# One stationary operand for the high and low parts of 64 tokens, a slot for each gated tile, and a new order of steps in a fused attention kernel

## The chip, the cores and the metric

The kernel runs on 1 core of one Trainium2 chip. The metric is the device time of one execution in microseconds, as the median of three runs. Work is spread over TensorE (PE in the profile, with its weight loads as PEld), VectorE (DVE), ScalarE (ACT), GpSimd (POOL) and the DMA engines, whose transfers are issued by SyncE (SP) and, for a few, by ACT.

## The reference, cut to what matters

Eight batches go through three blocks, each in float32:

- attention of 8 heads through 32 packed queries: `pp = softmax(p k^T) v`, then `softmax(q pp^T) pp`, for 576 tokens of 512 numbers (`x`);
- a gated MLP: `h = gelu(x w_in)`, halves `u` and `v`, `vn` = `v` normalised, `vs = w_sg vn + b_sg`, `x2 = x + (u * vs) w_out`;
- a mixture of 4 experts over causal attention: `logits = x2 w_gate`, the best two experts per token, `q, k, v = x2 wq, x2 wk, x2 wv` for each expert, and `out = sum of weight * softmax(q k^T) v wo`.

## The kernel before

**Tiles.** The 576 tokens are four tiles of 128 and one of 64. Factors are split into a rounded high part (float32r) and the low part that is left; a product takes three passes, high by high, high by low and low by high (`PASSES`). The weights of the third block are folded with `w_out`, so that `qk` and `vlog` come from the gated tiles `g` (four of 128 features, `m` = 0 to 3, with 576 tokens in each, times `w_qk` or `w_vg`) and from the packed attention `a2` (two halves `Q`, times `bd` or `bdv`, which `bdw` makes anew for each batch).

**Loops.** One batch after the other: `front(b)` makes `v` and its normalisation and `u`; `back(b)` makes `vs`, the gated tiles, `qk`, `vlog` and the gates, beside the attention steps of the batch before (S scores and softmax with E and N as its halves, T transposes, y and o the products) and the packed attention of the next one (K, s, n, a, p, P, Q, r). Batch 0 has a startup of its own (`ORDER`) and `first_back`, the others `later_back`; the last batch's attention is the tail of the program, in `back` at `b + 1 == B`.

**Order.** PE and SP run in the order of the program text (`tc.manual_schedule`). The startup's text orders all engines. Elsewhere DVE, ACT and POOL are ordered by a planner that simulates the program, except in blocks that name an engine. `prep_w_o` (loads, casts and splits the output weights) stands at the end of batch 0's back; its `lo_part` runs on POOL.

**Names that the change touches.** `gate_high` (L797) gives the gated tiles two by two a high and a low slot of tag `A`, and casts on ACT; `gate_low` (L805) subtracts on DVE. `vlog` (L861) makes, for a group of token tiles, 256 columns of values and 4 of logits: 12 matmuls from `g` (L871) and 6 from `a2` (L875) for each tile, a copy on ACT (L877) and one on DVE (L880), the latter twice for the tile of 64, to fill both halves of the partitions. `gates` (L882) follows the last `vlog`. `keep_last_q` (L855) copies on POOL what the last 64 queries need. `scores` of s is L392, its maximum L479 and exponential L481; `a1T` turns them (L501, copied at L503); `bdw` is L636. `v_pow` (L679) on POOL, `v_scale` (L683) and `v_low` (L698, L700) on DVE belong to the normalisation. The line of `lo_part` is L85, that of `act_copy` L82, both helpers. PSUM tiles are all of one tag, `pd`, with four slots.

Of the kernel before, what the change touches and what calls it, by code (L numbers as in the profile page):

```python
# [17 lines left out]
P = 128  # L18
# [8 lines left out]
def packed_attention_mlp_moe_kernel(  # L27
# [34 lines left out]

    NB = {"A": 4, "B": 10, "C": 4, "D": 12, "a": 3, "p": 2, "T": 4, "nat": 2, "t": 4, "v2": 1, "y": 1, "W": 2}
    NPS = 4
    BY = {"A": 1152, "B": 576, "C": 640, "D": 576, "a": 1152, "p": 576, "T": 512, "t": 576, "W": 2048}

    def slot(tag, dt=F32, w=None, name=None):
        t = sb.tile([P, BY[tag]], dt, tag=tag, name=name or ("s" + tag), bufs=NB[tag])
# [5 lines left out]
    def pd(name):  # L74

        return psum.tile([P, 2, 512], F32, tag="pd", name=name, bufs=NPS)
# [7 lines left out]
    def lo_part(eng, o, x, hi):  # L84
        eng.tensor_tensor(o, x, hi.bitcast(F32), op=OP.subtract)  # L85
# [548 lines left out]
        wp_out(b, f)  # L634

    def bdw(b):  # L636

        s = ST[b]
        pt = pd("bdq")
        per_head(b, pt, 512, w_of(b, "qk"))  # L640
        for Q in range(2):
            hi, lo = s["bd", Q] = [slot("B", F32R, 512, name="bdq") for _ in range(2)]
            nc.scalar.activation(hi, pt[:, Q, :], AF.Copy)
            lo_part(nc.vector, lo, pt[:, Q, :], hi)
        pt = pd("bdv")
        per_head(b, pt, 260, w_of(b, "vg"))
        t = [slot("B", F32R, 520, name="bdv").rearrange("p (q n) -> p q n", q=2) for _ in range(2)]
        nc.scalar.activation(t[0], pt[:, :, :260], AF.Copy)
        lo_part(nc.vector, t[1], pt[:, :, :260], t[0])
        for Q in range(2):  # L650
            s["bdv", Q] = [x[:, Q, :] for x in t]
# [144 lines left out]

    def gate_high(b, m):  # L797
        s = ST[b]
        if ("gt2", m // 2) not in s:
            s["gt2", m // 2] = (slot("A", F32R, name="gh"), slot("A", F32R, name="gl"))  # L800
        a = (m % 2) * S
        s["g", m] = [t[:, a:a + S] for t in s["gt2", m // 2]]
        nc.scalar.activation(two(s["g", m][0]), s["gt", m], AF.Copy)

    def gate_low(b, m):  # L805
        s = ST[b]
        hi, lo = s["g", m]
        lo_part(nc.vector, two(lo), s.pop(("gt", m)), two(hi))

    def qk(b, i):  # L810
        qk_mm(b, i)
# [48 lines left out]
    def vlog(b, cs):  # L860
        s = ST[b]  # L861
        if "v2" not in s:
            s["v2"] = sb.tile([P, NT, 256], F32, tag="v2", name="v2", bufs=NB["v2"])
            s["lg"] = small.tile([P, NT, E], F32, name="lg", bufs=2)
        n = TOK[cs[0]]
        k = len(cs)
        pt = pd("vlog")
        for ci, c in enumerate(cs):
            for m in range(4):
                for x, y in PASSES:  # L870
                    nc.tensor.matmul(pt[:n, ci, :260], s["g", m][x][:, c * P:c * P + n], W["w_vg"][y][:, m, :],  # L871
                                     start=(m, x, y) == (0, 0, 0), stop=False)
            for Q in range(2):
                for x, y in PASSES:
                    nc.tensor.matmul(pt[:n, ci, :260], s["a2", Q][x][:, c * P:c * P + n], s["bdv", Q][y],  # L875
                                     start=False, stop=(Q, x, y) == (1, 1, 0))
        nc.scalar.activation(s["v2"][:n, cs[0]:cs[0] + k, :], pt[:n, :k, :256], AF.Copy)  # L877

        for o in range(0, P, n):
            nc.vector.tensor_copy(s["lg"][o:o + n, cs[0]:cs[0] + k, :], pt[:n, :k, 256:260])  # L880

    def gates(b):  # L882
        s = ST[b]
# [1 line left out]
        T4 = [P, NT, E, E]  # L885
        other = lg[:, :, None, :].to_broadcast(T4)
        mine = lg[:, :, :, None].to_broadcast(T4)
        cmp = small.tile(T4, F32, name="cmp", bufs=1)
        eq = small.tile(T4, F32, name="eq", bufs=1)
        nc.vector.tensor_tensor(cmp, other, mine, op=OP.is_gt)  # L890
        nc.vector.tensor_tensor(eq, other, mine, op=OP.is_equal)
        nc.vector.tensor_tensor(eq, eq, tri[:, None, :, :].to_broadcast(T4), op=OP.mult)
# [224 lines left out]

    def first_back(b, do_all):
        tick(len(TURN))
        do_all("K0")  # L1120
        qk_gated(b, 0, True)
        do_all("s0 n0 K1 V")
        qk_gated(b, 2, True)
        do_all("s1 n1")
        bdw(b)
        weights(b + 1, ("in1", "in0"))
        do_all("a0")
        qk_packed(b, 0, False)
        qk_out(b, 0)
        do_all("a1 p0 Q0")  # L1130
        qk_packed(b, 2, False)
        qk_out(b, 2)
        keep_last_q(b, 0)
        do_all("P0")
        vlog(b, VT[2])
        do_all("p1 Q1 P1")
        vlog(b, VT[1])
        do_all("r")
        ahead(b + 2)

    def later_back(b, go, do_all, nxt):
        go("S1 S3")
        vs_tile(b, 0)
        vs_tile(b, 1)
        go("T1 T2 y0 S5 S4")
        vs_tile(b, 2)
        go("T3 o0 y1 T5 T4 S6 S7")
        vs_tile(b, 3)
# [30 lines left out]
    def back(b, go):  # L1179
# [16 lines left out]
        if b + 1 == B:  # L1196
            with tc.manual_schedule(engines={ET.DVE}):
                nxt("N8 N6")
                qk(b, 1)
                keep_last_q(b, 1)  # L1200
                nxt("E2 N4")
                qk_packed(b, 3, True)
                nxt("E0 N2")
                qk_gated(b, 3, False)
                qk_out(b, 3)
                nxt("N0 T8 T0 T2 E9 E1 T4 N9 E3 T6 N1 T9 y4 N3 T1 E5 y0 o4 T3 y1 N5 E7 o0 T5 y2 N7 o1 T7 y3 o2 o3")
            return
        qk(b, 1)
        keep_last_q(b, 1)
# [12 lines left out]
            qk_out(b, 3)  # L1222
            nxt("N0 N2")
        weights(b + 1, ("qk", "vg"))
        if b == 0:
            for j in range(2):
                prep_w_o(j)
        return nxt

    def ahead(b):  # L1230
# [294 lines left out]
```

## Time and profile before

| what | value |
|---|---|
| median of 3 runs | 844.61 us (844.15 to 848.43) |
| the profiled execution's own time | 844.43 us |
| its span, first to last instruction | 842.7 us |
| PE busy / PEld busy | 804.4 us (95%) / 695.5 us (83%) |
| DVE / ACT / POOL busy | 572.3 us (68%) / 431.1 us (51%) / 226.1 us (27%) |
| mean granted clock of TensorE | 0.992 |

A batch takes 94.5 us in its steady state. The busy time of PE counts matmuls whose durations overlap; where it is near the whole of a stretch, look in the timeline for the gaps that are left, which stand in brackets with what ended them. Times in the rows are microseconds from the span's start.

### The profile page before, as it was taken

The numbers are of one execution on the slowest core, as the hardware profiler recorded it, in microseconds if no ns is written. First come the engines' busy times: TensorE is split into PE (matmuls) and PEld (weight loads), VectorE is DVE, ScalarE is ACT, GpSimd is POOL, SyncE is SP. The second block draws the span as 40 slices with busy tenths as digits, with TensorE's granted clock in tenths as the row PEclk, the third lists the DMA queues.
The fourth block names the chain that finished last, engine by engine and source line by source line (L and its number), as shares of the span: only waits on it lengthen the run. The fifth ranks groups of instructions, "written<-read, shape, count | busy, mean of one in ns | idle before, by whom it ended". The sixth has DMA issues, their size and how long they took to land.

```text
span 842.7 us, 19253 instructions
## 1 busy us (share of the span) xinstructions
PE 804.4 (95%) x7523; PEld 695.5 (83%) x7523; DVE 572.3 (68%) x1359; ACT 431.1 (51%) x983; POOL 226.1 (27%) x301
## 2 busy tenths in 40 slices
PE   4689989999999999999999999999999999999988
PEld 2467778788889889888889889888889889888876
DVE  5999546776468846776468856776468856775374
ACT  3655432765347542665346542665346543665344
POOL 2457412403322322303322331303322322300000
PEclk9989999999999999999999999999999999999999
DMA  9977793617555374517565475617654470200001
GB/s 249 284 202 170 221 272 92 190 50 214 141 153 121 95 231 113 165 51 217 136 163 113 101 226 112 160 56 214 147 161 108 99 228 8 76 14 27 19 1 58
DMA packets 172710, 115.00 MB, mean 136 GB/s; under 512 B 119306, under 2 KB 153610, under 8 KB 169804
## 3 DMA queue, kind: packets, MB, share of 16 engines
q1 hardware_dynamic: 165644, 112.19, 49.7%
q10 hardware_dynamic: 6976, 1.58, 0.9%
q8 instruction: 60, 0.98, 0.5%
q14 instruction: 30, 0.25, 0.1%
HBM read 69.18 MB, written 29.63 MB: 117 GB/s over the span
## 4 chain that ended last, share of the span: by engine, by line
PE 59%; DVE 14%; ACT 4%; issue 3%; ACTq 0%
PE qk L828 10%; PE vlog L871 6%; PE vs L772 6%; PE y L1011 6%; PE qk L840 6%; PE o L1060 5%; PE aTp L982 4%; PE vlog L875 3%; PE sc L924 3%; DVE vg L683 2%; DVE bnst L671 2%; DVE vnl L698 2%; PE s L392 2%; PE sc L955 2%; DVE at L943 1%
## 5 line engine op out<-in xcount | busy, mean ns | idle before, releaser
L772 PE MATMUL vs<-w_sg,vnh 128*128 128x288 f32 x512 | 91.7, 301 | 3.4 <-ACT aT L82 1.9
L473 POOL COPY kT<-kp 128x576 uint16<-128x576 uint16 x56 | 50.2, 973 | 157.6 <-DMA kp<-turned_k 132.3
L828 PE MATMUL qk<-gh,w_qk 128*128 128x288 f32 x512 | 90.6, 299 | 0.0
L772 PEld LDWEIGHTS vs<-w_sg,vnh 128*128 128x128 f32 x512 | 74.5, 188 | 10.7 <-issue 3.9
L934 ACT ACTIVATE at<-sc,nm 128x256 f32<-128x256 f32 (+3 forms) x128 | 66.1, 524 | 32.4 <-DVE nm L928 28.6
L828 PEld LDWEIGHTS qk<-gh,w_qk 128*128 128x128 f32 x512 | 74.7, 188 | 9.3 <-issue 9.3
L82 ACT ACTIVATE aT<-aTp 128x512 f32<-128x512 f32 (+4 forms) x160 | 59.3, 434 | 21.1 <-PE aTp L982 17.7
L858 POOL CAST last_q<-qk 64x64 fp32r<-64x64 f32 x64 | 14.9, 232 | 178.4 <-ACT qk L848 101.6
L871 PE MATMUL vlog<-w_vg,gh 128*128 128x260 f32 (+1 forms) x320 | 60.5, 287 | 0.0
L473 POOL COPY qT<-qp 128x576 uint16<-128x576 uint16 x56 | 42.8, 833 | 62.0 <-DMA qp<-turned_q 61.9
L1011 PE MATMUL y<-aT,v 128*64 128x128 f32 (+2 forms) x960 | 57.7, 262 | 0.2 <-DVE y L85 0.2
L679 POOL TENSOR_TENSOR rstd<-rstd,mhalf 128x1 f32<-128x1 f32 x40 | 35.5, 894 | 83.2 <-DVE rstd L675 83.2
L1011 PEld LDWEIGHTS y<-aT,v 128*64 128x64 f32 (+1 forms) x960 | 46.7, 136 | 12.2 <-issue 7.3
L943 DVE TENSOR_SCALAR at<-at,sm,gw 128x256 f32<-128x256 f32 (+3 forms) x128 | 54.8, 470 | 1.6
L828 PE MATMUL qk<-gl,w_qk 128*128 128x288 f32 x256 | 54.8, 296 | 0.0
L772 PE MATMUL vs<-w_sg,vnl 128*128 128x288 f32 x256 | 54.7, 295 | 0.0
L928 DVE TENSOR_REDUCE nm<-sc 128x2 f32<-128x256 f32 (+3 forms) x64 | 52.0, 821 | 1.5
L871 PEld LDWEIGHTS vlog<-w_vg,gh 128*128 128x128 f32 (+1 forms) x320 | 47.2, 178 | 3.9 <-DVE lg L880 2.8
L1060 PE MATMUL o<-w_o,y 128*128 128x512 f32 x186 | 50.0, 404 | 0.0
L840 PE MATMUL qk<-a2h,bdq 128*128 128x288 f32 x256 | 46.8, 305 | 0.0
L982 PE MATMUL aTp<-ident,at 128*128 128x128 f32 x320 | 43.6, 274 | 2.7 <-DVE at L943 2.3
L871 PE MATMUL vlog<-w_vg,gl 128*128 128x260 f32 (+1 forms) x160 | 45.1, 282 | 0.0
(237 smaller groups left out, 1922.9 us busy)
## 6 DMA issues: line engine op xcount, KB each, us to landing
w_in<-kept_in SPq DMA_DIRECT2D x14, 1024.0 KB
w_qk<-kept_qk SPq DMA_DIRECT2D x8, 1024.0 KB
turned_k<-kx SPq DMA_DIRECT2D x28, 288.0 KB
turned_q<-qx SPq DMA_DIRECT2D x28, 288.0 KB
kp<-turned_k SPq DMA_DIRECT2D x56, 144.0 KB
qp<-turned_q SPq DMA_DIRECT2D x56, 144.0 KB
out_dram<-ot SPq DMA_DIRECT2D x31, 256.0 KB
v<-in_v_dram SPq DMA_DIRECT2D x56, 128.0 KB
```

Source lines behind the costliest of these rows:

```text
L82: nc.scalar.activation(o, i, AF.Copy, scale=scale)
L473: nc.gpsimd.tensor_copy(w[:, i], t[:, i].rearrange("p h n -> p (h n)"))
L772: nc.tensor.matmul(pt[:, h, :], s["vn", c][x][:, cols], w_sg[y][:, c, hs(h)], start=(c, x, y) == (0, 0, 0), stop=False)
L828: nc.tensor.matmul(o[:, h, :], W["w_qk"][y][:, m, cols], s["g", m][x][:, hs(h)], start=first and (m, x, y) == (0, 0, 0), stop=not first an ...
L840: nc.tensor.matmul(o[:, h, :], s["bd", Q][y][:, cols], s["a2", Q][x][:, hs(h)], start=first and (Q, x, y) == (0, 0, 0), stop=not first and ...
L871: nc.tensor.matmul(pt[:n, ci, :260], s["g", m][x][:, c * P:c * P + n], W["w_vg"][y][:, m, :], start=(m, x, y) == (0, 0, 0), stop=False)
L928: nc.vector.tensor_reduce(nm, pt[:, :, :L], axis=AX.X, op=OP.max, negate=True)
L934: nc.scalar.activation(ats[e][:, :L], pt[:, e, :L], AF.Exp, bias=nm[:, e:e + 1], accum_out=sm[:, e:e + 1])
L943: nc.vector.tensor_scalar(ats[e][:, :L], ats[e][:, :L], sm[:, e:e + 1], s["w"][:, j, 2 * pr + e:2 * pr + e + 1], op0=OP.mult, op1=OP.mult)
L982: nc.tensor.transpose(pt[:, e, c * P:c * P + P], ats[e][:, c * P:c * P + P], ident)
L1011: nc.tensor.matmul(pt[64 * e:64 * e + 64, pr * w:pr * w + w], s["v2"][:m, c, col:col + D], s["aT", pr, e, j][c][:m, :], start=c == 0, stop ...
L1060: nc.tensor.matmul(pt, ys[:, pr, x, :], W["w_o"][y][:, pr, :], start=i == 0, stop=i == 5)
```

## The change

It has six parts.

1. **One slot per gated tile.** Each `m` gets one `A` slot of 1216 numbers: the high part (576), room for 64, the low part (576). `gate_low` copies the low part's last 64 columns into that room, on ACT, so that the last 64 tokens' high and low parts lie side by side.
2. **The 64-token tile of `vlog`.** One matmul with those 128 columns as stationary operand gives high by high and low by high at once, in the two halves of the partitions; a second one, with the 64 high columns, gives high by low. From `g` it is 8 matmuls in place of 12. The halves are then added: a copy on ACT and an addition on DVE for the values, a copy and an addition on DVE for the logits, and a copy on POOL fills the other half.
3. **`first_back`** has a new order: `V` ahead of `K0`, both score steps together, `bdw` in two parts, with DVE in the text's order for the middle of it.
4. **`prep_w_o`** moves from the end of batch 0's back to ahead of the steps that fetch batch 2.
5. **`later_back`** orders ACT as T1, T2, then the gating of the second `vs` tile.
6. **The tail** has N0 ahead of `qk_out(b, 3)`, and T2, T4 and the E steps earlier.

Beside these, `gates` takes its two scratch tiles from the tag `rem`.

```diff
@@ -62,7 +62,7 @@
 
     NB = {"A": 4, "B": 10, "C": 4, "D": 12, "a": 3, "p": 2, "T": 4, "nat": 2, "t": 4, "v2": 1, "y": 1, "W": 2}
     NPS = 4
-    BY = {"A": 1152, "B": 576, "C": 640, "D": 576, "a": 1152, "p": 576, "T": 512, "t": 576, "W": 2048}
+    BY = {"A": 1216, "B": 576, "C": 640, "D": 576, "a": 1152, "p": 576, "T": 512, "t": 576, "W": 2048}
 
     def slot(tag, dt=F32, w=None, name=None):
         t = sb.tile([P, BY[tag]], dt, tag=tag, name=name or ("s" + tag), bufs=NB[tag])
@@ -634,7 +634,10 @@
         wp_out(b, f)
 
     def bdw(b):
-
+        bdw_qk(b)
+        bdw_vg(b)
+
+    def bdw_qk(b):
         s = ST[b]
         pt = pd("bdq")
         per_head(b, pt, 512, w_of(b, "qk"))
@@ -642,6 +645,9 @@
             hi, lo = s["bd", Q] = [slot("B", F32R, 512, name="bdq") for _ in range(2)]
             nc.scalar.activation(hi, pt[:, Q, :], AF.Copy)
             lo_part(nc.vector, lo, pt[:, Q, :], hi)
+
+    def bdw_vg(b):
+        s = ST[b]
         pt = pd("bdv")
         per_head(b, pt, 260, w_of(b, "vg"))
         t = [slot("B", F32R, 520, name="bdv").rearrange("p (q n) -> p q n", q=2) for _ in range(2)]
@@ -796,16 +802,15 @@
 
     def gate_high(b, m):
         s = ST[b]
-        if ("gt2", m // 2) not in s:
-            s["gt2", m // 2] = (slot("A", F32R, name="gh"), slot("A", F32R, name="gl"))
-        a = (m % 2) * S
-        s["g", m] = [t[:, a:a + S] for t in s["gt2", m // 2]]
+        t = s["gx", m] = slot("A", F32R, name="g")
+        s["g", m] = [t[:, :S], t[:, S + 64:]]
         nc.scalar.activation(two(s["g", m][0]), s["gt", m], AF.Copy)
 
     def gate_low(b, m):
         s = ST[b]
         hi, lo = s["g", m]
         lo_part(nc.vector, two(lo), s.pop(("gt", m)), two(hi))
+        act_copy(s["gx", m][:, S:S + 64], lo[:, 512:].bitcast(F32))
 
     def qk(b, i):
         qk_mm(b, i)
@@ -867,17 +872,28 @@
         pt = pd("vlog")
         for ci, c in enumerate(cs):
             for m in range(4):
+                if n < P:
+                    for y, k in ((0, P), (1, n)):
+                        nc.tensor.matmul(pt[:k, 0, :260], s["gx", m][:, 512:512 + k], W["w_vg"][y][:, m, :],
+                                         start=(m, y) == (0, 0), stop=(m, y) == (3, 0), skip_group_check=True)
+                    continue
                 for x, y in PASSES:
                     nc.tensor.matmul(pt[:n, ci, :260], s["g", m][x][:, c * P:c * P + n], W["w_vg"][y][:, m, :],
                                      start=(m, x, y) == (0, 0, 0), stop=False)
             for Q in range(2):
                 for x, y in PASSES:
                     nc.tensor.matmul(pt[:n, ci, :260], s["a2", Q][x][:, c * P:c * P + n], s["bdv", Q][y],
-                                     start=False, stop=(Q, x, y) == (1, 1, 0))
-        nc.scalar.activation(s["v2"][:n, cs[0]:cs[0] + k, :], pt[:n, :k, :256], AF.Copy)
-
-        for o in range(0, P, n):
-            nc.vector.tensor_copy(s["lg"][o:o + n, cs[0]:cs[0] + k, :], pt[:n, :k, 256:260])
+                                     start=False, stop=(Q, x, y) == (1, 1, 0), skip_group_check=n < P)
+        if n < P:
+            v4, l4 = s["v2"][:n, 4, :], s["lg"][:, 4, :]
+            nc.scalar.activation(v4, pt[n:, 0, :256], AF.Copy)
+            nc.vector.tensor_tensor(v4, v4, pt[:n, 0, :256], op=OP.add)
+            nc.vector.tensor_copy(l4[:n], pt[n:, 0, 256:260])
+            nc.vector.tensor_tensor(l4[:n], l4[:n], pt[:n, 0, 256:260], op=OP.add)
+            nc.gpsimd.tensor_copy(l4[n:], l4[:n])
+            return
+        nc.scalar.activation(s["v2"][:, cs[0]:cs[0] + k, :], pt[:, :k, :256], AF.Copy)
+        nc.vector.tensor_copy(s["lg"][:, cs[0]:cs[0] + k, :], pt[:, :k, 256:260])
 
     def gates(b):
         s = ST[b]
@@ -885,8 +901,7 @@
         T4 = [P, NT, E, E]
         other = lg[:, :, None, :].to_broadcast(T4)
         mine = lg[:, :, :, None].to_broadcast(T4)
-        cmp = small.tile(T4, F32, name="cmp", bufs=1)
-        eq = small.tile(T4, F32, name="eq", bufs=1)
+        cmp, eq = [small.tile([P, 2 * D], F32, tag="rem", name=n, bufs=2)[:, :NT * E * E].rearrange("p (c i j) -> p c i j", c=NT, i=E) for n in ("cmp", "eq")]
         nc.vector.tensor_tensor(cmp, other, mine, op=OP.is_gt)
         nc.vector.tensor_tensor(eq, other, mine, op=OP.is_equal)
         nc.vector.tensor_tensor(eq, eq, tri[:, None, :, :].to_broadcast(T4), op=OP.mult)
@@ -1117,32 +1132,39 @@
 
     def first_back(b, do_all):
         tick(len(TURN))
-        do_all("K0")
+        do_all("V K0")
         qk_gated(b, 0, True)
-        do_all("s0 n0 K1 V")
-        qk_gated(b, 2, True)
-        do_all("s1 n1")
-        bdw(b)
-        weights(b + 1, ("in1", "in0"))
-        do_all("a0")
-        qk_packed(b, 0, False)
-        qk_out(b, 0)
-        do_all("a1 p0 Q0")
-        qk_packed(b, 2, False)
-        qk_out(b, 2)
+        do_all("K1")
+        with tc.manual_schedule(engines={ET.DVE}):
+            do_all("s0 s1")
+            bdw_qk(b)
+            do_all("n0 n1")
+            qk_gated(b, 2, True)
+            qk_packed(b, 0, False)
+            do_all("a0 a1")
+            qk_out(b, 0)
+            bdw_vg(b)
+            weights(b + 1, ("in1", "in0"))
+            qk_packed(b, 2, False)
+            qk_out(b, 2)
         keep_last_q(b, 0)
-        do_all("P0")
+        do_all("p0 Q0 p1 Q1")
         vlog(b, VT[2])
-        do_all("p1 Q1 P1")
+        do_all("P0 P1")
         vlog(b, VT[1])
         do_all("r")
+        for j in range(2):
+            prep_w_o(j)
         ahead(b + 2)
 
     def later_back(b, go, do_all, nxt):
         go("S1 S3")
         vs_tile(b, 0)
-        vs_tile(b, 1)
-        go("T1 T2 y0 S5 S4")
+        vs_mm(b, 1)
+        with tc.manual_schedule(engines={ET.Activation}):
+            go("T1 T2")
+            vs_out(b, 1)
+        go("y0 S5 S4")
         vs_tile(b, 2)
         go("T3 o0 y1 T5 T4 S6 S7")
         vs_tile(b, 3)
@@ -1202,8 +1224,9 @@
                 qk_packed(b, 3, True)
                 nxt("E0 N2")
                 qk_gated(b, 3, False)
+                nxt("N0")
                 qk_out(b, 3)
-                nxt("N0 T8 T0 T2 E9 E1 T4 N9 E3 T6 N1 T9 y4 N3 T1 E5 y0 o4 T3 y1 N5 E7 o0 T5 y2 N7 o1 T7 y3 o2 o3")
+                nxt("T8 T2 T4 E9 E1 N9 T6 T0 E3 N1 T9 E5 y4 N3 T1 y0 E7 o4 T3 N5 y1 o0 T5 N7 y2 o1 T7 y3 o2 o3")
             return
         qk(b, 1)
         keep_last_q(b, 1)
@@ -1222,9 +1245,6 @@
             qk_out(b, 3)
             nxt("N0 N2")
         weights(b + 1, ("qk", "vg"))
-        if b == 0:
-            for j in range(2):
-                prep_w_o(j)
         return nxt
 
     def ahead(b):
```

## Rows read from the trace of the kernel before

**Rows 1.** Busy time of each engine in two stretches: batch 0's back, one whole batch.

```profile
core 0: us, PE busy (x) PEld busy (x) DVE busy (x) ACT busy (x) POOL busy (x), PEclk, DMA share, GB/s
105.10:150.50 45.40, 41.70 (x479) 35.94 (x478) 24.21 (x64) 14.81 (x35) 13.08 (x22) 0.96 0.67 170
...
245.00:339.50 94.50, 94.05 (x920) 82.95 (x919) 64.88 (x159) 49.30 (x114) 25.31 (x36) 1.00 0.54 143
```

**Rows 2.** Timeline of PE, batch 1's 64-token tile of `vlog`: start, us, engine, line.

```profile
228.89 0.46 PE L871 MATMUL vlog<-w_vg,gh 128*64 128x260 f32 x2
...
230.38 0.40 PE L875 MATMUL vlog<-bdv,a2h 128*64 128x260 f32 x2
```

**Rows 3.** Groups by line and form, ACT and DVE: busy us, mean ns of one.

```profile
L426 ACT ACTIVATE ppT<-ppT 128x128 f32<-128x128 f32 x16 | 3.8, 275 | 5.3 <-PE ppT L421 5.2
...
L85 DVE TENSOR_TENSOR y<-y 128x256 fp32r<-128x256 f32 x32 | 13.4, 419 | 17.4 <-ACT y L1024 17.4
...
L880 DVE COPY lg<-vlog 64x4 f32<-64x4 f32 x16 | 2.4, 150 | 1.3 <-ACT v L877 1.2
```

**Rows 4.** Timeline of PE, back of batch 0: the three gaps, in brackets.

```profile
115.20 0.67 PE L605 MATMUL bdv<-w_vg,ppT 64*32 64x260 f32 x16 [0.93 <-ACT a L481]
...
117.96 1.09 PE L501 MATMUL a1T<-ident,a 128*128 128x128 f32 x4 [2.09 <-DVE bdq L85]
...
128.56 0.30 PE L421 MATMUL ppT<-ident,pp 128*128 128x128 f32 x1 [0.69 <-DVE pp L416]
```

**Rows 5.** Busy time in two stretches behind the longest gap; columns as in Rows 1.

```profile
118.00:120.00 2.00, 2.00 (x9) 2.00 (x10) 1.11 (x2) 0.00 (x0) 0.00 (x0) 0.50 1.00 291
...
120.00:122.00 2.00, 2.00 (x21) 1.83 (x23) 0.02 (x1) 0.46 (x1) 0.00 (x0) 0.79 0.99 389
```

**Rows 6.** Timeline of DVE and PE at the end of the startup.

```profile
101.96 4.49 DVE L85 TENSOR_TENSOR gl<-vs,gh 128x576 fp32r<-128x576 f32 x4
...
105.28 0.76 PE L828 MATMUL qk<-gh,w_qk 128*128 128x288 f32 x4
```

**Rows 7.** Timeline of POOL, DVE and PE, the front of batch 1.

```profile
147.83 3.37 POOL L85 TENSOR_TENSOR a2l<-a2f,a2h 128x576 fp32r<-128x576 f32 x4
...
157.80 3.31 POOL L85 TENSOR_TENSOR w_o<-wst,w_o 128x512 fp32r<-128x512 f32 x2 [6.61 <-ACT w_o L82]
...
158.25 1.72 DVE L683 SCALAR_TENSOR_TENSOR vg<-vg,mv,g_bc 128x512 f32<-128x512 f32 x1
...
164.29 0.74 DVE L683 SCALAR_TENSOR_TENSOR vg<-vg,mv,g_bc 128x512 f32<-128x512 f32 x1
...
152.77 0.62 PE L661 MATMUL v<-wph,a2l 128*128 128x512 f32 x2
...
162.96 0.79 PE L742 MATMUL u<-a2h,wph 128*128 128x288 f32 x4 [0.74 <-ACT u L749]
...
172.06 0.54 PE L776 MATMUL vs<-w_sg,vnh 128*128 128x288 f32 x2 [1.38 <-DVE vnh L700]
```

**Rows 8.** Timeline of ACT and PE around the third `vs` tile of batch 2.

```profile
272.27 0.69 ACT L803 ACTIVATE gh<-gt 128x576 fp32r<-128x576 f32 x1 [0.83 <-DVE gt L795]
...
272.86 0.64 ACT L82 ACTIVATE aT<-aTp 128x256 f32<-128x256 f32 x2
...
273.55 0.80 PE L772 MATMUL vs<-w_sg,vnh 128*128 128x288 f32 x4 [0.32 <-ACT aT L82]
```

**Rows 9.** Timeline of PE, the tail of the last batch: three of its gaps.

```profile
813.00 0.93 PE L982 MATMUL aTp<-ident,at 128*128 128x128 f32 x6 [1.73 <-DVE at L943]
...
818.79 0.74 PE L996 MATMUL aTp<-ident,at 128*128 128x128 f32 x5 [0.72 <-DVE at L968]
...
833.24 1.06 PE L982 MATMUL aTp<-ident,at 128*128 128x128 f32 x8 [0.56 <-DVE at L943]
```

**Rows 10.** Timeline of DVE, POOL and ACT, end of batch 3's back.

```profile
426.49 0.23 DVE L890 TENSOR_TENSOR cmp<-lg 128x80 f32<-128x80 f32 x1
...
430.18 0.51 POOL L858 CAST last_q<-qk 64x64 fp32r<-64x64 f32 x2 [7.86 <-ACT qk L848]
...
435.61 1.02 ACT L621 ACTIVATE wph<-wp 128x1024 fp32r<-128x1024 f32 x1 [1.38 <-PE wp L605]
```

## The prediction

> **What bounds the kernel now.** I read the stretches first: in a whole batch PE is busy for 94.05 of 94.50 us at full clock, and in batch 0's back for 41.70 of 45.40 at 0.96 [rows 1]. So a batch in the steady state ends when PE has issued its matmuls, and only three things shorten the program: fewer matmuls, a gap of PE that goes, or a stretch at the low clock that goes. DVE, ACT and POOL have room on average; they count where PE waits for them. Then I read PE's timeline for its gaps. Outside the startup they sit in four places: batch 0's back, batch 1's front, once per batch ahead of the third `vs` tile, and the tail. The change reaches into each of them.
>
> **The change, part by part.** The sum is made against the profiled execution, 844.43 us (span 842.7); the median of the runs is 0.18 above it.
>
> *Matmuls.* Twelve matmuls of the 64-token tile start between 228.89 and 230.38 [rows 2], 0.124 us each; they are issued back to back, so 4 fewer are worth 0.50 us in each of 8 batches: **-4.0**. The wider stationary operand (128 columns for half of them) loads beside the matmul before. Nothing ties this to a wait, since the tile's followers are PE work.
>
> *What the halves cost.* Per batch ACT gets 4 copies of 128x64; the nearest is a 128x128 copy at 0.275 us [rows 3], so at most 1.1 us. DVE gets an addition of 64x256 (at most the 0.42 us of 128x256) and a small addition at about 0.15 in place of a copy [rows 3]. POOL gets one copy of 64x4, under the 0.26 us of a 64x64 cast [rows 10]. The 64 tokens' values are read a whole batch later, and ACT idles 45 of 94.5 us [rows 1], so I take nothing for them. If the cover goes, 0.4 us of DVE and 0.3 of ACT reach the gates, which is a rival below. The PSUM slot is held some 0.6 us longer; the next tile of `vlog` and two score tiles come before its turn.
>
> *Startup.* Here the text orders all engines, so the 4 copies stand in ACT's queue. The four subtractions follow each other from 101.96, 1.12 us each, in the order 1, 3, 0, 2, and PE begins with tile 0 at 105.28 [rows 6]. The cast of tile 3 now waits behind the copy of tile 1's low part, so the second subtraction starts after one subtraction, one copy (0.275) and one cast (0.69 [rows 8]) instead of after the subtraction: 0.97 late, and tile 0's low part is done at 106.3 where PE wants it near 105.8. POOL's copies, beside which these subtractions are slow, end at the same time, which gives some back: **+0.4**, between 0 and 1.0.
>
> *Batch 0's back.* PE waits 0.93, 2.09 and 0.69 us [rows 4], together 3.7. The first two are one knot: `bdw` needs what the second score step's exponential releases, and the a1 transposes need a PSUM slot that DVE frees late. Behind it the clock is granted at 0.50 for 2 us and at 0.79 for two more [rows 5], which loses 2 x 0.50 + 2 x 0.21 = 1.4. In the new order 24 + 12 `qk` matmuls lie between the scores and the transposes, and both score steps lie ahead of `bdw`, so softmax and splitting run beside matmuls. What is late next: `bdv` needs a slot that the first transposes' copy (about 0.7 us) frees, with only four more transposes beside it, so 0.4 stays. **-4.7** (3.7 + 1.4 - 0.4). `V` ahead of `K0` puts three more loads ahead of the `q` planes on SP, `weights` now waits for the later `bdv`, and the transposes of batch 2 start a few us later; POOL's joins and batch 1 have that much room. Bounds: 0 if a load is late, -5.1 if nothing stays.
>
> *Batch 1's front.* POOL works 3.31 us on `w_o` from 157.80 on, ahead of the normalisation's `v_pow`; PE then waits 0.74 for a PSUM slot that ACT frees late and 1.38 for `vnh` [rows 7]. In the other batches neither gap is there. With `w_o` moved these go: **-2.1**. Moved, its 2 loads, 2 casts and 2 subtractions lie in batch 0's back, where POOL is busy for 13.1 of 45.4 us [rows 1]. SP waits there until the packed products have read the tiles that `w_o` is loaded into. Bounds: -2.6 (with the smaller slips) to +1.6 (below).
>
> *Ahead of the third `vs` tile.* PE waits 0.32 us for the PSUM slot that the copy of T2's transposes frees; that copy starts at 272.86, behind a cast that waited for DVE until 272.27 [rows 8]. With T1 and T2 first, the copies fit into the ACT gap before the cast, and the tile follows its forerunner. There are six such gaps, of 0.32 to 0.33 us, in batches 2 to 7: **-1.9**. Queued behind the cast now is the low part's copy, which waits for DVE's subtraction; the copy of `y0` comes after it and is wanted some us later.
>
> *Tail.* PE's first waits for N0 (1.73), then for the last tile's norm (0.72), then for N7 (0.56) [rows 9], 3.0 in all. N0 ahead of `qk_out`'s subtraction uses DVE time that was idle, and T8, T2, T4 need nothing that is late; E5 and E7 earlier make N5 and N7 early. What is late next: T9 follows E9, E1, T6, T0 and E3, about 2.2 us of PE work, while the chain of maximum, exponential and norm behind E9 takes over 3 us, so about 1 us of wait stays: **-2.0**, between 0 and -3.4.
>
> Sum: -4.0 + 0.4 - 4.7 - 2.1 - 1.9 - 2.0 = -14.3, that is 844.43 - 14.3 = 830.1, and with the 0.2 by which the median lies above that execution, **830.3 us**.
>
> **A rule weighed.** In batch 1 a DVE operation with two operands in SBUF took 1.72 us beside POOL's subtraction and 0.74 alone [rows 7]. The Trainium skill, "SBUF — State Buffer", section "Who interferes with whom", says of such a pair that whoever starts first holds the shared port for the whole instruction and the other blocks. The row agrees: 0.98 us lost. It speaks against the move of `w_o`, and is the third rival.
>
> **The rivals.** *Batch 0's order gives nothing:* DMA is already at 0.99 of its engines around 120 us [rows 5], and `bdq` now wants its weights 3 us earlier; if it waits as long as the knot did, the 4.7 are lost and the time is 835.0. For it: the share. Against it: the weights are issued ahead of all that moved.
>
> *Only the matmuls count:* the planner, which simulates the program, orders DVE and ACT differently with 32 more copies, and each gap that goes comes back elsewhere. Then 844.6 - 4.0 = 840.6. Against it: the gaps have different causes, and three of the four places are ordered by hand.
>
> *`w_o` collides in its new place:* its two subtractions, 3.31 us on POOL, come ahead of the subtraction in the packed softmax of batch 1 (r) and hold up DVE's operations beside it by 0.98 each. The low part of `a2`, four operations on POOL from 147.83 for 3.37 us, was done 1.57 us before PE used it at 152.77 [rows 7]; 3.31 + 2 x 0.98 - 1.57 = 3.7 late gives 834.0.
>
> *The gates come late, and the kernel is slower:* `gates` now waits for POOL's copy of the 64 tokens' logits. POOL's queue there holds `last_q`, which waits for ACT until 430.18. If the planner puts the new copy behind it, the gates start at about 430.18 + 0.51 + 0.26 = 430.95 and not at 426.49 [rows 10], 4.5 us late; DVE's and ACT's queues stand behind them, and the exponentials ahead of `wph` have only 1.38 us before that starts at 435.61. That leaves 3.1 us for PE in each of 7 batches: 830.3 + 21.7 = 852.0. It decides from 2.6 us per batch on (848.8 - 830.3 over 7). Against it: POOL is idle for 7.86 us ahead of `last_q` [rows 10], and the tile of 64 is done before the last two.
>
> **How the numbers follow.** Forecast 0.60; batch 0 gives nothing 0.13; `w_o` collides 0.09; only the matmuls 0.11; gates late 0.07. About 0.5% (4.2 us) is what a measurement of this kernel can tell from no change. Faster by more than that (below 840.4): the first three and half of the fourth, 0.88; within it: the other half and a little of the last, 0.07; slower: 0.05. The range reaches down to 826.0, where batch 0, front and tail lose all their waits (-0.4, -0.5, -1.4) and the startup nothing (-0.4), with the rest for smaller slips, and up to 839.5, which takes in both middle rivals together and leaves out what is most of the last two.
>
> **What would show it.** In the changed profile: 8 matmuls from `g` for the tile of 64, in about 1.0 us; batch 0's back some 5 us shorter with its clock near 1.00; no POOL work on `w_o` in batch 1's front and no gap before its `vnh` matmuls; no gap before the third `vs` tile, and a batch of 93.7 us; T8, T2 and T4 without a gap, one before T9, none before T7. The forecast is wrong if a batch still takes 94.5 us or more, if PE waits for `bdq`'s weights, or if the gates' first comparison starts behind `last_q`.

## The result, and the profile after

The changed kernel takes **839.98 us** (median; 835.7 to 842.6) against 847.2 us for the kernel before in the same session: ratio 0.9914, 95% interval 0.9887 to 0.9942. It is faster, as forecast, by 7.2 us in place of 14.3, and the time lies half a microsecond above the range. The prediction counted from 844.61 us, the median of the first three runs of the kernel before; over seven runs it is 847.2. Of the 9.7 us between the forecast 830.3 and 839.98 this accounts for 2.6, and the gain that stayed out for 7.1. The profiled execution took 838.03 us (span 836.3) with the clock at 0.996.

Where the 6.4 us between the two profiled executions lie, measured on PE's timeline from the first `v` matmul of one batch to that of the next (with five of the third row the sum is -6.7; the first gated `qk` starts at the same time in both, and what follows the last matmul is 0.3 longer):

| stretch | before | after | difference | forecast |
|---|---|---|---|---|
| first gated `qk` to batch 1's `v` | 46.04 | 42.41 | -3.6 | -4.8 |
| batch 1 | 96.80 | 93.75 | -3.1 | -2.6 |
| batches 2 to 6, each | 94.54 | 94.79 | **+0.25** | **-0.82** |
| batch 7's `v` to the last matmul's end | 118.84 | 117.58 | -1.3 | -2.8 |

So the places of the program that come once behave nearly as forecast. The steady batch, which comes again and again, became longer although it has fewer matmuls. These are the ends of its periods, in PE's timeline of the changed kernel:

```profile
147.70 0.63 PE L667 MATMUL v<-wph,a2h 128*128 128x512 f32 x2
241.45 0.63 PE L667 MATMUL v<-wph,a2h 128*128 128x512 f32 x2
336.27 0.63 PE L667 MATMUL v<-wph,a2h 128*128 128x512 f32 x2
...
715.38 0.63 PE L667 MATMUL v<-wph,a2h 128*128 128x512 f32 x2
```

The 64-token tile is shorter: its 8 matmuls from `g` start between 412.27 and 413.33, 1.06 us, where the 12 took 1.49 [rows 2]. The gap of 0.32 us ahead of the third `vs` tile [rows 8] is gone. In its place PE waits inside `y0`, once in each of batches 2 to 7 (PE's timeline):

```profile
359.44 0.44 PE L1026 MATMUL y<-aT,v 128*64 128x128 f32 x4
360.60 0.60 PE L1026 MATMUL y<-aT,v 128*64 128x128 f32 x4 [0.71 <-ACT aT L82]
...
412.27 1.23 PE L877 MATMUL vlog<-w_vg,g 128*128 128x260 f32 x8
413.33 0.40 PE L885 MATMUL vlog<-bdv,a2h 128*64 128x260 f32 x2
```

The second half of `y0` waits for T1's copies. The engine that makes them, and the one that this engine waits for, in the timelines of ACT and then of DVE:

```profile
358.41 0.69 ACT L807 ACTIVATE g<-gt 128x576 fp32r<-128x576 f32 x1 [0.83 <-DVE gt L801]
360.12 0.26 ACT L82 ACTIVATE g<-g 128x64 fp32r<-128x64 f32 x1 [1.03 <-DVE g L85]
360.29 0.98 ACT L82 ACTIVATE aT<-aTp 128x128 f32<-128x128 f32 x4
...
357.62 0.75 DVE L801 TENSOR_TENSOR gt<-vs,u 128x576 f32<-128x576 f32 x1
358.29 0.16 DVE L955 TENSOR_SCALAR sm<-sm 128x2 f32<-128x2 f32 x1
358.49 0.17 DVE L956 RECIPROCAL sm<-sm 128x2 f32<-128x2 f32 x1
358.69 0.74 DVE L958 TENSOR_SCALAR at<-at,sm,gw 128x256 f32<-128x256 f32 x2
359.34 0.75 DVE L85 TENSOR_TENSOR g<-gt,g 128x576 fp32r<-128x576 f32 x1
```

The planner has put tile 0's low-part copy, the one of 0.26 us, ahead of the four copies of T1 and T2. ACT stands idle for 1.03 us until DVE's subtraction is done, and the four copies stand behind. That T1's could have run at once is seen in the experiments, where they start 0.03 us behind the cast. One row of the groups by line and form says the same for the whole program: the 32 copies are busy for 8.2 us, and ACT was idle for 21.1 us directly ahead of them.

```profile
L82 ACT ACTIVATE g<-g 128x64 fp32r<-128x64 f32 x32 | 8.2, 257 | 21.1 <-DVE g L85 21.1
```

In batch 0's back the gaps of [rows 4] and the low clock of [rows 5] are gone; three shorter waits are new (PE's timeline). In the tail, where the waits of [rows 9] are gone, three others stand:

```profile
105.29 0.77 PE L833 MATMUL qk<-g,w_qk 128*128 128x288 f32 x4
106.86 2.92 PE L833 MATMUL qk<-g,w_qk 128*128 128x288 f32 x20 [0.80 <-DVE g L85]
...
111.53 1.09 PE L605 MATMUL bdq<-w_qk,ppT 64*32 64x512 f32 x16 [0.62 <-DMA w_qk<-kept_qk]
...
118.82 0.67 PE L605 MATMUL bdv<-w_vg,ppT 64*32 64x260 f32 x16 [0.35 <-DVE a1t L503]
...
810.44 0.62 PE L939 MATMUL sc<-qk 64*128 64x256 f32 x6 [0.66 <-ACT at L976]
811.53 0.74 PE L1011 MATMUL aTp<-ident,at 128*128 128x128 f32 x5 [0.48 <-ACT aT L82]
816.41 0.60 PE L1026 MATMUL y<-aT,v 128*64 128x128 f32 x4 [0.93 <-ACT aT L82]
```

### The profile page after: what moved, and what is told of

It is laid out like the page before. It is cut to its first block, busy times and chain, and to the rows that moved or that the text cites. A ratio compares the mean times of both kernels' runs of the same rounds, so it can differ in the third digit from the quotient of the medians.

```text
span 836.3 us, 19244 instructions
## 1 busy us (share of the span) xinstructions
PE 802.0 (96%) x7491; PEld 693.1 (83%) x7491; DVE 574.4 (69%) x1367; ACT 437.0 (52%) x1015; POOL 228.2 (27%) x309
## 4 chain that ended last, share of the span: by engine, by line
PE 68%; DVE 15%; DMA 7%; ACT 4%; issue 4%; SPq 2%; ACTq 0%; DVEq 0%
PE qk L833 11%; PE y L1026 7%; PE vs L778 6%; PE qk L845 6%; PE vlog L881 6%; PE o L1075 5%; PE sc L939 4%; PE aTp L997 3%; PE vlog L885 3%; DVE vg L689 3%; DVE bnst L677 2%; DVE vnl L704 2%; PE s L392 2%; PE sc L970 2%; DVE at L958 1%
## 5 line engine op out<-in xcount | busy, mean ns | idle before, releaser
L833 PEld LDWEIGHTS qk<-g,w_qk 128*128 128x128 f32 x768 | 103.8, 188 | 10.7 <-issue 8.4
L833 PE MATMUL qk<-g,w_qk 128*128 128x288 f32 x768 | 110.5, 298 | 0.8 <-DVE g L85 0.8
L1026 PE MATMUL y<-aT,v 128*64 128x128 f32 (+2 forms) x960 | 60.5, 263 | 5.2 <-ACT aT L82 5.2
L881 PE MATMUL vlog<-w_vg,g 128*128 128x260 f32 x384 | 52.0, 284 | 0.0
L881 PEld LDWEIGHTS vlog<-w_vg,g 128*128 128x128 f32 x384 | 48.3, 189 | 0.8 <-issue 0.7
L778 PEld LDWEIGHTS vs<-w_sg,vnl 128*128 128x128 f32 x256 | 41.1, 188 | 0.0
L939 PE MATMUL sc<-qk 64*128 64x128 f32 (+3 forms) x384 | 40.2, 338 | 0.7 <-ACT at L976 0.7
```

The source lines that it names most:

```text
L778: nc.tensor.matmul(pt[:, h, :], s["vn", c][x][:, cols], w_sg[y][:, c, hs(h)], start=(c, x, y) == (0, 0, 0), stop=False)
L833: nc.tensor.matmul(o[:, h, :], W["w_qk"][y][:, m, cols], s["g", m][x][:, hs(h)], start=first and (m, x, y) == (0, 0, 0), stop=not first an ...
L939: nc.tensor.matmul(pt[:, e, :L], qs[x][r, j * P:L], ks[y][r, :L], start=i == 0, stop=i == 2)
L1026: nc.tensor.matmul(pt[64 * e:64 * e + 64, pr * w:pr * w + w], s["v2"][:m, c, col:col + D], s["aT", pr, e, j][c][:m, :], start=c == 0, stop ...
```

## The experiments

Two theories stood at the start. *Copy*: the time is lost to where the low part's copy stands in ACT's queue. *Planner*: 32 more instructions make the planner order DVE and ACT differently, and each gap that goes comes back elsewhere, copies or not. Ratios are against the kernel before.

**copy_after_T**: tile 0's copy behind T1 and T2 on ACT (the diff is to the changed kernel, as the next four are).

```diff
...
-        vs_tile(b, 0)
+        vs_mm(b, 0)
+        gate_mul(b, 0)
+        gate_high(b, 0)
+        gate_low(b, 0, False)
         vs_mm(b, 1)
         with tc.manual_schedule(engines={ET.Activation}):
             go("T1 T2")
+            gate_room(b, 0)
             vs_out(b, 1)
```

> The changed kernel with one ACT instruction moved: the copy of gated tile 0's low part comes behind T1's and T2's copies, not ahead of them; all that is computed stays. Copy theory (T1's and T2's copies wait on ACT for that copy, which waits for DVE's subtraction, and y0 on PE waits for them): the 0.71 us gap in y0 goes in each of batches 2 to 7 and the batch falls from 94.80 to about 94.0 us, the whole by some 5 us to 833. Planner theory (the batch is late because DVE now multiplies vs by u behind the norms): the gap moves to the scores or the third vs tile behind it, the batch stays within 0.2 us of 94.8.

Measured: 835.15 us, ratio 0.987 (0.9851 to 0.9889), 93.91 us a batch, no wait in `y0`. The same copies on the same engine, one of four moved behind T1 and T2, give back 0.88 us a batch.

**copy_on_pool**: the copies of batches 1 to 7 on POOL.

```diff
-        act_copy(s["gx", m][:, S:S + 64], lo[:, 512:].bitcast(F32))
+        if b:
+            nc.gpsimd.tensor_copy(s["gx", m][:, S:S + 64], lo[:, 512:].bitcast(F32))
+        else:
+            act_copy(s["gx", m][:, S:S + 64], lo[:, 512:].bitcast(F32))
```

> The changed kernel with the four copies of the low parts on POOL in place of ACT for all batches but the first. Copy theory: as in the run before, about 94.0 us a batch, the whole near 833 us. Planner theory: 94.6 to 94.8 us a batch. If POOL's copies hold up its rstd operations or joins, a new gap shows in the front and the batch is longer than 94.8.

Measured: 832.61 us, ratio 0.984 (0.9822 to 0.9858), 93.90 us a batch. The timelines of ACT and POOL in this version:

```profile
357.56 0.69 ACT L807 ACTIVATE g<-gt 128x576 fp32r<-128x576 f32 x1 [0.83 <-DVE gt L801]
358.28 0.45 ACT L82 ACTIVATE aT<-aTp 128x128 f32<-128x128 f32 x2
359.14 0.66 ACT L82 ACTIVATE aT<-aTp 128x256 f32<-128x256 f32 x2 [0.41 <-PE y L1029]
...
359.38 0.24 POOL L814 CAST g<-g 128x64 fp32r<-128x64 f32 x1 [8.53 <-PE y L1029]
```

T1's copies follow the cast at once. POOL had been idle for 8.53 us, and PE waits for nothing behind its copy. The theory of the copy holds: two versions that only take the copy out of ACT's way are 4.8 and 7.4 us faster than the changed kernel by their medians. From batch 1's `v` to the last matmul's end the profiled executions take 680.01 and 679.98 us in place of 685.26, 5.3 less in both; what the medians differ by beyond that lies ahead of it. The planner theory keeps a smaller part, which `gate_first` shows below.

**no_act_block**: the change without the block that orders ACT as T1, T2, then the gating.

```diff
-        vs_mm(b, 1)
-        with tc.manual_schedule(engines={ET.Activation}):
-            go("T1 T2")
-            vs_out(b, 1)
-        go("y0 S5 S4")
+        vs_tile(b, 1)
+        go("T1 T2 y0 S5 S4")
```

> The changed kernel without the ACT order T1, T2, gating of tile 1. If the order is worth the 0.32 us that I counted, the gap ahead of the third vs tile is back and the batch is 0.3 us longer than the changed kernel's 94.80, with the gap in y0 still there in part (T1's copies still stand behind the copy of tile 0). If the order gives nothing or costs, the batch is 94.5 to 94.8.

Measured: 838.16 us, 0.9904 (0.9879 to 0.993), 94.78 us a batch, the same 0.7 us in `y0`. The block orders T1 and T2 against tile 1's gating. It says nothing of tile 0's copy, which the planner puts ahead with it or without it.

**vlog_alone**: the kernel before with only the 64-token tile, its copies and slots; that is, every order undone.

```diff
...
-        do_all("V K0")
+        do_all("K0")
...
-        nxt("T8 T2 T4 E9 E1 N9 T6 T0 E3 N1 T9 E5 y4 N3 T1 y0 E7 o4 T3 N5 y1 o0 T5 N7 y2 o1 T7 y3 o2 o3")
+        nxt("N0 T8 T0 T2 E9 E1 T4 N9 E3 T6 N1 T9 y4 N3 T1 E5 y0 o4 T3 y1 N5 E7 o0 T5 y2 N7 o1 T7 y3 o2 o3")
...
```

> The kernel before with the slots and the 64-token tile of the change alone, all orders as before. Matmul theory: 4 matmuls fewer show as 0.45 to 0.5 us in each batch, 94.0 us. Copy theory: the copy of tile 0 stands ahead of T1's copies here too, so y0 waits and the batch is 94.5 to 95.0 us; the startup has the 0.8 us wait for tile 0's low part; the whole lies within 3 us of the kernel before.

Measured: 846.76 us, ratio 1.0003 (0.9987 to 1.0018), 94.78 us a batch with 0.70 to 0.72 us of wait in `y0`. By itself this part of the change is worth nothing: what its matmuls save, its copy gives back.

**orders_only**: the other half, the new orders with the old 64-token tile.

```diff
-    BY = {"A": 1216, "B": 576, "C": 640, "D": 576, "a": 1152, "p": 576, "T": 512, "t": 576, "W": 2048}
+    BY = {"A": 1152, "B": 576, "C": 640, "D": 576, "a": 1152, "p": 576, "T": 512, "t": 576, "W": 2048}
...
-        act_copy(s["gx", m][:, S:S + 64], lo[:, 512:].bitcast(F32))
...
```

> The kernel before with the changed orders alone: the old 64-token tile with its 12 matmuls and no copies. Terms as forecast (-4.7 batch 0's back, -2.1 batch 1's front, -1.9 third vs tile, -2.0 tail = -10.7, from 846.8 of these days' runs of before): 836.1 us, batch period 94.2 us (94.53 less 0.32). Terms as the changed kernel's trace shows them (-3.1, -2.1, -1.9, -1.55 = -8.65): 838.1 us, same period. Rival (the 0.32 us gap was taken away by the copies' place in ACT's queue and not by the order of T1 and T2): period 94.5 us, gap still there, about 840 us.

Measured: **835.48 us**, ratio 0.9871 (0.9856 to 0.9885), 94.13 us a batch and no gap ahead of the third `vs` tile: 11.0 us faster than before, where the forecast's terms give 10.7. That they meet so closely is in part luck: between the two profiled executions it is 9.1 us (-3.0 in batch 0's back, where `bdq` waits 1.24 us for its weights, -2.6 in batch 1, -2.0 in batches 2 to 6, -2.0 behind them, and 0.4 lost ahead of the first gated `qk`), nearer to the second sum. Half of the change is better than the whole of it. The block on ACT also does what the forecast said, as long as no copy stands ahead of it.

**undo_back0**: on `copy_on_pool`, batch 0's back in its old order.

```diff
-        do_all("V K0")
+        do_all("K0")
         qk_gated(b, 0, True)
-        do_all("K1")
-        with tc.manual_schedule(engines={ET.DVE}):
-            do_all("s0 s1")
-            bdw_qk(b)
...
+        do_all("s0 n0 K1 V")
+        qk_gated(b, 2, True)
+        do_all("s1 n1")
+        bdw(b)
...
```

> The version with the copies on POOL (832.6 us), with batch 0's back in its old order and all else kept. Forecast's term: 4.7 us slower, 837.3 us, first gated qk to the first v matmul 47.6 us instead of 42.9. The size that the traces show (46.04 less 0.5 for the matmuls against 42.9): 2.6 us slower, 835.2 us. Rival (the new order only moves waits, which batch 1's front then takes): within 0.5 us of 832.6.

Measured: the stretch takes 48.15 us (from 103.28 to 151.43) in place of 42.93, 5.22 longer, where 4.7 were forecast; the 103.8 and 47.7 of the next expectation are these two in that trace. The median is 842.38 us (836.3 to 845.6), about 4.5 more than the stretch explains. **undo_back0_again** is the same version in another execution:

> The version with the copies on POOL and batch 0's old order once more, for its spread (836.3 to 845.6 us): if it lies in the startup, the first gated qk matmul starts later than 103.8 us by as much as the time is above 836.3, and from there to the first v matmul it is 47.7 us again. If it lies in batch 0's back, that stretch is longer.

PE's timeline in the first execution and, behind the dots, in the second:

```profile
103.28 0.77 PE L836 MATMUL qk<-g,w_qk 128*128 128x288 f32 x4
104.44 2.92 PE L836 MATMUL qk<-g,w_qk 128*128 128x288 f32 x20 [0.39 <-DVE g L85]
128.67 0.30 PE L421 MATMUL ppT<-ident,pp 128*128 128x128 f32 x1 [1.44 <-DVE pp L416]
151.43 0.63 PE L667 MATMUL v<-wph,a2h 128*128 128x512 f32 x2
...
106.49 0.77 PE L836 MATMUL qk<-g,w_qk 128*128 128x288 f32 x4
108.25 4.44 PE L836 MATMUL qk<-g,w_qk 128*128 128x288 f32 x20 [0.99 <-DVE g L85]
134.30 0.30 PE L421 MATMUL ppT<-ident,pp 128*128 128x128 f32 x1 [2.75 <-DVE pp L416]
157.06 0.63 PE L667 MATMUL v<-wph,a2h 128*128 128x512 f32 x2
```

In the second execution (841.98 us) the stretch took 50.57 us and began 3.21 later. Both supposed places have a part. The stretch is 2.42 us longer: 0.60 are a longer wait for the startup's subtraction, 1.52 the 20 matmuls behind it, and 1.31 the wait for `pp`, which is 0.69 in [rows 4]; about 1.0 comes back behind the wait of 2.09 us, where the matmuls up to `pp` take 9.65 us and not 10.67. The old back is thus not only longer but less steady.

**undo_w_o**: on `copy_on_pool`, `w_o` prepared in batch 1's front.

```diff
-        for j in range(2):
-            prep_w_o(j)
         ahead(b + 2)
...
         weights(b + 1, ("qk", "vg"))
+        if b == 0:
+            for j in range(2):
+                prep_w_o(j)
```

> The version with the copies on POOL (832.6 us), with w_o prepared in batch 1's front again. Forecast's term: 2.1 us slower, 834.7 us, batch 1 takes 95.8 us instead of 93.7, with gaps of 0.74 and 1.38 us ahead of the u and vs matmuls. By the run with the 64-token tile alone, whose gaps there were 0.74 and 0.68: 1.4 us slower, 834.0 us. If the move costs batch 0 as much as it saves batch 1 (a collision in its new place): no difference.

Measured: batch 1 takes 95.71 us in place of 93.71, 2.0 longer, where 2.1 were forecast; 0.25 of it is a longer wait for `wpl` at its start, the rest arises around the two waits below. The timelines of POOL, DVE and PE:

```profile
153.38 3.00 POOL L85 TENSOR_TENSOR w_o<-wst,w_o 128x512 fp32r<-128x512 f32 x2 [6.31 <-ACT w_o L82]
...
153.39 1.84 DVE L689 SCALAR_TENSOR_TENSOR vg<-vg,mv,g_bc 128x512 f32<-128x512 f32 x1
155.22 1.72 DVE L689 SCALAR_TENSOR_TENSOR vg<-vg,mv,g_bc 128x512 f32<-128x512 f32 x1
158.93 0.74 DVE L689 SCALAR_TENSOR_TENSOR vg<-vg,mv,g_bc 128x512 f32<-128x512 f32 x1
...
158.69 0.79 PE L748 MATMUL u<-a2h,wph 128*128 128x288 f32 x4 [0.58 <-ACT u L755]
167.09 0.53 PE L782 MATMUL vs<-w_sg,vnh 128*128 128x288 f32 x2 [0.68 <-DVE vnh L706]
```

DVE's operations beside POOL's two subtractions take 1.84 and 1.72 us, and 0.74 without them. The Trainium skill, "SBUF — State Buffer", section "Who interferes with whom", says that a DVE instruction with two operands in SBUF contends with a GpSimd instruction that reads SBUF. These rows agree. The time is 836.58 us, 4.0 and not 2.0 more: the tail, too, is 1.35 us longer, with a wait of 1.41 us in `y1` (817.66) that the other version doesn't have. An edit in batch 1 has changed the planner's order 650 us later: two `aT` copies stand later in ACT's queue there. Batch 0's back is 1.67 us shorter in this execution (41.26 us), but only the 0.21 us for which PE waits on `w_o`'s subtraction in `copy_on_pool` belong to the move; the rest is mostly the startup's wait of 0.81, which is gone here, and the wait at `bdq`, 0.41 in place of 0.85.

**waits_moved**: on `copy_on_pool`, three waits at once.

```diff
...
-            bdw_qk(b)
-            do_all("n0 n1")
-            qk_gated(b, 2, True)
+            qk_gated(b, 2, True, (0,))
+            bdw_qk(b)
+            do_all("n0 n1")
+            qk_gated(b, 2, None, (1, 2, 3))
...
+        for m in range(4):
+            gate_room(b, m)
         keep_last_q(b, 0)
...
-                nxt("T8 T2 T4 E9 E1 N9 T6 T0 E3 N1 T9 E5 y4 N3 T1 y0 E7 o4 T3 N5 y1 o0 T5 N7 y2 o1 T7 y3 o2 o3")
+                nxt("T8 T2 T4 E9 E1 N9 T6 T0 E3 N1 T9 y4 N3 T1 E5 y0 E7 o4 T3 N5 y1 o0 T5 N7 y2 o1 T7 y3 o2 o3")
```

> The version with the copies on POOL (832.6 us) with three more edits: batch 0's copies stand behind its back's matmuls and not between its gate casts; six matmuls of the third qk block stand ahead of bdq; E5 stands between T1 and y0 again. Theory (each wait has its own cause): the startup wait of 0.81 us falls to about 0.1, the 0.85 ahead of bdq to 0 to 0.3, the 0.93 in the tail's y0 to 0, together -2.3 us, 830.3 us. Rival (PE only waits elsewhere, above all for E5's follower in the tail): 832 to 833 us.

Measured on PE's timeline: the startup's wait is gone, `bdq` waits 0.31, and the stretch takes 41.43 us in place of 42.93; the tail is 0.8 shorter (its 0.93 has become 0.21 and 0.37). Together -2.3, as expected, though it is not shown that moving the copies did the startup's part: in `undo_w_o` that wait is gone too, with the copies where they were. The median is 831.65 us (828.2 to 833.5), ratio 0.9821 (0.979 to 0.9852): by its median 1.0 better than `copy_on_pool`, which the spread of its runs does not separate.

**tile_on_pool**: on the kernel before, the 64-token tile alone with its copies on POOL. Its diff to `vlog_alone` is the one of `copy_on_pool`.

> The kernel before with the new 64-token tile alone (old orders throughout), its copies on POOL in batches 1 to 7. Forecast's term for the matmuls (-0.5 a batch, copies free): 846.5 - 4.0 = 842.5 us, batch period 94.0 us, no wait in y0. Rival (the gap ahead of the third vs tile and a later gated product on DVE take part of it): period 94.2 to 94.5 us, 844 to 846 us; nothing at all if the copies on ACT were not the cause of the run with the tile alone.

Measured: 844.9 us, ratio 0.9985 (0.9961 to 1.001), 94.47 us a batch. The rival came in. The wait in `y0` is gone, but ahead of the third `vs` tile PE now waits 0.47 us, not 0.32:

```profile
275.15 0.79 PE L772 MATMUL vs<-w_sg,vnh 128*128 128x288 f32 x4 [0.47 <-ACT aT L82]
```

Of the 0.43 us that the matmuls save, 0.07 are left. What the tile saves is only had together with the orders.

**gate_first**: on `waits_moved`, tile 0's gated product ahead of the norms on DVE.

```diff
-        go("S1 S3")
-        vs_tile(b, 0)
+        with tc.manual_schedule(engines={ET.DVE}):
+            go("E1 E3")
+            vs_mm(b, 0)
+            gate_mul(b, 0)
+            go("N1 N3")
+        gate_high(b, 0)
+        gate_low(b, 0)
         vs_mm(b, 1)
```

> The run waits_moved (831.7 us, batch period 93.92 us) with the gated product of tile 0 written out by hand ahead of the two norm steps on DVE, as DVE had it in the kernel before. Theory (0.25 us a batch are lost in the score step ahead of the third vs tile, because PE waits there for a slot that the gated product of tile 1 frees, late on DVE behind the norms): period 93.67 us, 830.2 us. Rival (the norms come late instead and the T1 transposes wait): period 93.9 us or more, 831.7 us or slower.

What led to it is a wait that PE's gaps above 0.2 us don't show, since it sits inside a score step; the timeline of weight loads of `copy_on_pool` has it:

```profile
453.12 0.47 PEld L942 LDWEIGHTS sc<-qk 64*128 64x128 f32 x6 [0.17 <-issue]
453.91 0.47 PEld L942 LDWEIGHTS sc<-qk 64*128 64x128 f32 x6 [0.31 <-DVE gt L801]
```

Measured: 93.67 us a batch, to the digit what was expected, and the 93.7 of the prediction: once the copy is out of ACT's way and DVE has its old order, the whole of the forecast saving is there; from batch 1's `v` to the last matmul's end 677.74 us in place of 679.19. The median is 831.54 us, ratio 0.9828 (0.9793 to 0.9864), no better than `waits_moved`: its profiled execution began the first gated `qk` 0.44 later and waited 0.86 us for `w_o`'s subtraction on POOL in batch 0's back.

**after_again**: the changed kernel as it stands.

> The changed kernel once more, for its startup: if the spread of its runs (835.7 to 842.6 us) lies in the loads and conversions ahead of the first gated qk matmul, batch periods are 94.8 us again and the time differs from the profiled 838.0 by as much as that matmul's start does from 105.3 us.

Measured: 840.44 us, 2.41 more than the first profile. The first gated `qk` starts 0.70 later, the wait in it is 0.20 longer, and the 20 matmuls behind it take 4.44 us and not 2.92. PE's timeline, and the busy time by stretch (PE, PEld, DVE, ACT, POOL, granted clock, DMA share, GB/s):

```profile
105.99 0.78 PE L833 MATMUL qk<-g,w_qk 128*128 128x288 f32 x4
107.76 4.44 PE L833 MATMUL qk<-g,w_qk 128*128 128x288 f32 x20 [1.00 <-DVE g L85]
```

```profile
106.00:108.00 2.00, 1.00 (x7) 0.77 (x6) 2.00 (x3) 0.51 (x3) 2.00 (x2) 1.00 0.73 153
108.00:110.00 2.00, 2.00 (x12) 2.00 (x12) 1.90 (x3) 1.98 (x5) 0.41 (x1) 0.63 0.90 293
110.00:112.00 2.00, 2.00 (x10) 1.98 (x9) 0.00 (x0) 0.56 (x1) 0.00 (x0) 0.52 0.95 341
112.00:114.00 2.00, 1.38 (x40) 0.56 (x40) 1.04 (x2) 0.25 (x1) 0.00 (x0) 1.00 0.91 273
```

The clock was granted at 0.63 and 0.52 over four microseconds, so the lower of its two levels, 1.2 GHz, for most of them.

From batch 1's `v` to the last matmul's end both executions take the same (685.24 and 685.26 us), so the difference of these two is made ahead of it.

## Why the prediction was wrong, and where it was right

**The step that failed** is the one on what the halves cost: "The 64 tokens' values are read a whole batch later, and ACT idles 45 of 94.5 us, so I take nothing for them." It asked who waits for the copies' result, and nobody does. It did not ask who stands behind the copy on ACT while the copy waits for DVE, though the step on the third `vs` tile came close ("Queued behind the cast now is the low part's copy, which waits for DVE's subtraction"): it saw tile 1's copy, whose follower is not pressed, and not tile 0's, which the hand-written block leaves to the planner. Behind that one stand T1's copies, and `y0` needs these at once. The size: 94.79 us a batch against 93.91 and 93.90 with the copy out of the way, 0.9 us in each of six batches, 5.3 of the 7.1 us by which the gain fell short. ACT's idle time on average was no cover, because the copy makes ACT idle: 21.1 us for 8.2 us of work. Two of the signs that the prediction names for its being wrong came: a batch above 94.5 us, and a wait of PE for `bdq`'s weights.

**Matmuls**, -4.0: mis-sized, and not free of conditions. The 8 take 1.06 us, so 0.43 are saved and not 0.50. "Nothing ties this to a wait" was wrong: alone, with the copies on POOL, 0.07 us a batch are left of it; with the orders 0.23 (94.13 to 93.90); with DVE's gated product put back in its old place, where `orders_only` has it too, 0.46 (to 93.67). The rest is waited for in two places. In the score step ahead of the third `vs` tile it is the planner's doing: on DVE it has put the gated products behind the norms, and PE waits there for the slot that one of them frees. Ahead of that tile itself PE comes earlier, and the slot that ACT frees does not.

**Batch 0's back**, -4.7: right in the main; undone alone it costs 5.22 us in one execution and 7.64 in the other. The 1.4 us of it that were counted for the low clock are no fixed price: `vlog_alone` has the old order and the same wait of 2.09 us, and its clock stays at 1.00. The net of -3.6 is smaller because `bdq` waits 0.62 us for its weights, the first rival's cause at about an eighth of its size, and for the startup.

**Startup**, +0.4: the wait is 0.80, inside the bounds and twice the term. Its mechanism was right: the second subtraction waits 0.90 us for the cast behind the copy, where 0.97 were counted. What was mis-sized is POOL's part. The rows of DVE and POOL, in the changed kernel and then in `undo_w_o`:

```profile
104.44 3.62 DVE L85 TENSOR_TENSOR g<-vs,g 128x576 fp32r<-128x576 f32 x3 [0.90 <-ACT g L807]
99.15 8.36 POOL L473 COPY kT<-kp 128x576 uint16<-128x576 uint16 x7
...
104.66 2.44 DVE L85 TENSOR_TENSOR g<-vs,g 128x576 fp32r<-128x576 f32 x3 [0.90 <-ACT g L807]
99.37 5.83 POOL L473 COPY kT<-kp 128x576 uint16<-128x576 uint16 x5
```

The three subtractions take 1.2 us longer beside POOL's copies, and in `undo_w_o`, where these end at 105.20, PE does not wait. That a stretch at the low clock can follow a wait there, as in [rows 4, 5], was left out; the matmuls in it took 1.5 us longer in one of two executions.

**Batch 1's front**, -2.1: right, 2.0 when undone. The collision that the third rival feared is small where `w_o` stands now: no wait in the changed kernel, 0.21 and 0.86 us in two of the versions with copies on POOL.

**Ahead of the third `vs` tile**, -1.9: right for the orders alone (0.41 us a batch, where 0.32 were counted). **Tail**, -2.0: from `qk(3)`'s gated matmuls on it is 1.55 shorter; T9's wait (0.48) is half of what was expected, but E3's slot (0.66) and `y0` (0.93, where E5 no longer stands between) were not foreseen.

**The rivals.** *Gates late* is refuted: POOL's copy of the logits ran at 130.60, the first comparison at 139.64, `last_q` at 141.21, and in every later batch they come in this order too. *Only the matmuls count* named the right time, 840.6 against 839.98, but by chance: the planner did reorder DVE, at a price of 0.25 us a batch (`gate_first`), but the once-only gaps stayed away, and the copies' own place on ACT cost the most. `vlog_alone` and `orders_only` show it the other way round: everything but the matmuls counted.

Not settled is what moves the startup itself: the first gated `qk` began between 103.3 and 108.2 us in the profiled executions of twelve versions. No run took the loads or the conversions ahead of it apart.

## What to carry to other kernels

An instruction put on an engine costs not its duration but the time that it blocks its queue, its own wait included (here a copy of 0.26 us cost 0.88 us a batch): ask what it waits for, and what stands behind it, before calling an idle engine a cover; a small copy belongs on the engine whose followers can wait. Where a planner orders that engine, an order written by hand for two steps does not hold a third from being put ahead of them. And a saving on the busy engine is worth only what the next wait leaves of it, so measure the parts alone and together: here one part alone was worth nothing, the other part alone was worth more than both.

## What the runs showed of the hardware that was not expected

The same wait was followed by different clocks. The startup's wait of 0.80 us was followed by the clock at 1.00, and the one of 1.00 us, in another execution of the same kernel, by 0.63 and 0.52 over the next four microseconds. Behind the 2.09 us of batch 0's old order it was at 0.50 and 0.79 for two microseconds each in the kernel before [rows 5], and at 0.50 for three such stretches, from 116 to 122 us, in `undo_back0`. In `vlog_alone`, whose wait there is the same 2.09 us, it stayed at 1.00, as it did behind a startup's wait of 1.08 us in `copy_after_T`. Two stretches behind the 2.09 us, in `undo_back0` and then in `vlog_alone` (columns as above):

```profile
118.00:120.00 2.00, 2.00 (x10) 2.00 (x10) 0.39 (x1) 0.00 (x0) 0.00 (x0) 0.50 0.99 410
...
119.00:121.00 2.00, 1.61 (x13) 1.64 (x14) 1.59 (x3) 0.00 (x0) 0.00 (x0) 1.00 1.04 199
```

A short wait of PE at full clock can therefore have a price that one profile need not show.
